# One PSUM accumulation and one quotient per attention head, in a fused attention and channel-mix kernel

## The chip, the cores and the metric

The kernel runs on one core of a Trainium2 chip. The metric is the device time of one execution in microseconds; lower is better. Engines are named as the profile names them: PE (TensorE matmuls) with PEld (its weight loads), DVE (VectorE), ACT (ScalarE), POOL (GpSimd) and SP (SyncE, which issues the DMAs).

## The reference

Attention for 8 batches of 8 heads, with 1152 keys of width 64. Neighbouring queries are averaged in twos, so each head has 576 queries. The heads of a batch, side by side, are the 576 x 512 input of a gated channel mix.

```python
def _attn_ref(q, k, v):                       # each 8 x 8 x 1152 x 64
    q_pool = q.reshape(B, H, S // 2, 2, D).mean(axis=3)
    scores = 1.0 / np.sqrt(D) * np.matmul(q_pool, k.transpose(0, 1, 3, 2))
    scores = scores - np.max(scores, axis=-1, keepdims=True)
    attn = np.exp(scores)
    attn = attn / (np.sum(attn, axis=-1, keepdims=True) + 1e-09)
    return np.matmul(attn, v)

def _moe_ref(x, mu_k, mu_r, w_k, w_v, w_r):   # x: 8 x 576 x 512
    x_prev = x shifted by one row of the sequence, zeros first
    xk = mu_k * x + (1.0 - mu_k) * x_prev
    xr = mu_r * x + (1.0 - mu_r) * x_prev
    k = np.maximum(xk @ w_k, 0.0)             # 512 x 1024
    v = k * k @ w_v                           # 1024 x 512
    return 1.0 / (1.0 + np.exp(-(xr @ w_r))) * v
```

## The kernel before

The 64 heads are worked off one after the other. `prep` loads k, q and v of a head and splits each into two float16 parts (tiles kn, qn, vt, vb). `block` handles 96 queries, six blocks to a head: scores of all 1152 keys into one of three PSUM tiles `s` (PE, L356), the maximum over keys (DVE `mx` L363, PE L366, DVE `mb` L369, PE L371, ACT L374), a second scores product that corrects the first and takes the maximum off (PE, L380), the exponential into `pf` (ACT, L386), and its low part into `pl` (POOL, L388).

`window` multiplies the exponentials with v. A group is 128 queries; the five groups of a head start at 0, 128, 256, 352 and 448 (the last ones overlap). Each group is 27 matmuls that accumulate in 65 columns of PSUM tile `a`, one bank: nine of L404, nine of L406 (high parts) and nine of L411 (low parts). Column 64 becomes the sum of the exponentials, the divisor. Before the change the five groups form three windows, `WIN`: groups 0 and 1 are issued after block 2, groups 2 and 3 after block 4, group 4 after block 5. Each window ends with a quotient of its own on DVE: `den` = divisor plus a guard (L427), its reciprocal (L429), and the product `xb` (L430). After the odd head of a pair each window is also turned: PE transposes one 128 x 128 block per group into bank `a` (L440), and ACT copies the result to `xt` (L444), the channel mix's input. Bank `a` is one buffer: the next group, quotient or transpose that uses it waits for the last.

`ff` is the channel mix for 256 rows at a time: `mix` makes xk and xr (ACT L510, DVE L513 and L518), then come its matmuls (PE, L538). A pair of heads is one of the four pieces of 128 channels over which its first products sum, so it starts as the pairs of a batch are turned, and runs interleaved with the heads of later batches. `weights` splits the three weight matrices, 20 pieces, by four DVE instructions each (L471 to L475); in the trace the last of them runs at 202 us.

Nothing is issued where it is written. `op` records each step with its engine, an assumed duration, the buffers it reads and writes, and a key; `Issue.run` then plays the whole list forwards and backwards with these durations and latencies and fixes one order per engine. So a change in a few steps changes the order everywhere.

Of the kernel before, what the change touches and what calls it, by code (L numbers as in the profile page):

```python
# [10 lines left out]
F32 = mybir.dt.float32  # L11
# [22 lines left out]
GUARD = 1e-9 * math.exp(SHIFT) * 2.0 ** -40  # L34
# [6 lines left out]
O_MAX, O_EXP, O_REST, O_AV, O_EVAC, O_TURN = -6.0, 0.0, 3.0, 14.0, 6.0, 4.0  # L41
# [134 lines left out]
def kernel(  # L176
# [65 lines left out]
    vb = bufs("vb", NV, [P, NC, D + 2], F16)  # L242
    pf = const.tile([P, NC, TQ], I32, name="pf")
    pl = const.tile([P, NC, TQ], F16, name="pl")
    mx, mb = bufs("mx", 3, [P, QN], F16), bufs("mb", 3, [P, 1], F16)
    den, xb = bufs("den", 2, [P, 2], F32), bufs("xb", NW, [P, 2, 2, D], F32)
    xt = bufs("xt", 3, [P, NG, TQ + 1], F32)
    xm = {n: const.tile([P, NG, T], F32, name=f"x{n}") for n in "kr"}
    xl = {n: const.tile([P, NG, T], F16, name=f"xl{n}") for n in "kr"}
# [10 lines left out]
    a_b = psum.tile([P, 512], F32, name="a")  # L260
# [130 lines left out]

    def window(n, w, t):

        b, h = divmod(n, H)
        g, hh = divmod(h, 2)
        starts, r1, _ = WIN[w]
        m = len(starts)
        jv = n % NV
        VN = D + 1
        vk = [(x, jv, c0) for x in ("vt", "vtl") for c0 in (0, 5)]  # L400

        def hi(a0, rows, c0, c1, first):
            for c in range(c0, c1):
                nc.tensor.matmul(a_b[:, a0:a0 + VN], half(pf, F16, 1)[:, c, rows], vt[jv][:, c, D:D + VN],  # L404
                                 start=(first and c == 0), stop=False, skip_group_check=True)
                nc.tensor.matmul(a_b[:, a0:a0 + D], half(pf, F16, 1)[:, c, rows], vt[jv][:, c, 0:D],  # L406
                                 start=False, stop=False, skip_group_check=True)

        def lo(a0, rows, c0, c1):
            for c in range(c0, c1):  # L410
                nc.tensor.matmul(a_b[:, a0:a0 + VN], pl[:, c, rows], vb[jv][:, c, 0:VN],  # L411
                                 start=False, stop=(c == NC - 1), skip_group_check=True)

        for k_, r0 in enumerate(starts):
            js = range(r0 // QN, (r0 + P - 1) // QN + 1)
            a0, rows = k_ * VN, slice(r0, r0 + P)
            for c0 in (0, 3, 6):
                op("PE", 3 * 0.0595, lambda a0=a0, rows=rows, c0=c0, first=(k_ == 0): hi(a0, rows, c0, c0 + 3, first),
                   r=vk + [("pf", j) for j in js] + ([("a",)] if c0 or k_ else []), w=[("a",)], key=t)
            for c0, c1 in ((0, 5), (5, NC)):  # L420
                op("PE", (c1 - c0) * 0.030, lambda a0=a0, rows=rows, c0=c0, c1=c1: lo(a0, rows, c0, c1),
                   r=[("vb", jv)] + [("pl", j) for j in js] + [("a",)], w=[("a",)], key=t)

        u = a_b[:, 0:m * VN].rearrange("p (k x) -> p k x", k=m)
        z = iss.nx = 1 - getattr(iss, "nx", 0)
        dz, xz = den[z][:, 0:m], xb[w][:, 0:m]
        op("DVE", 0.13, lambda: nc.vector.tensor_scalar(dz, u[:, :, D], GUARD, None, op0=ALU.add),  # L427
           r=[("a",)], w=[("den", z)], key=t + O_EVAC)
        op("DVE", 0.1, lambda: nc.vector.reciprocal(dz, dz), r=[("den", z)], w=[("den", z)], key=t + O_EVAC)  # L429
        op("DVE", 0.13 + m * D / 960, lambda: nc.vector.tensor_tensor(  # L430
            xz[:, :, hh], u[:, :, 0:D], dz.unsqueeze(2).broadcast_to([P, m, D]), op=ALU.mult),
           r=[("den", z), ("a",)], w=[("xb", w, hh)], key=t + O_EVAC)
        if hh == 0:
            return
        q0 = r1 - starts[0]
        qe = starts[-1] + P - starts[0]

        def turned():
            for k_, r0 in enumerate(starts):
                nc.tensor.transpose(a_b[:, r0 - starts[0]:r0 - starts[0] + P],  # L440
                                    xz[:, k_].rearrange("p h d -> p (h d)"), ident)

        op("PE", 0.11 * m, turned, r=[("xb", w, 0), ("xb", w, 1)], w=[("a",)], key=t + O_TURN)
        op("ACT", 0.051 + (qe - q0) / 1200, lambda: nc.scalar.copy(  # L444
            xt[b % 3][:, g, 1 + r1:1 + r1 + qe - q0], a_b[:, q0:qe]),
           r=[("a",)], w=[("xt", b % 3, g, w)], key=t + O_TURN)
# [49 lines left out]
    def mix(w, t0, t1, key, dk):  # L496

        m, o = mu[w]
        n = t1 - t0
        hi = top(xm[w])  # L500
        for c in range(NG):
            t = t0
            while t < t1:
                b = t // TQ
                e = min(t1, (b + 1) * TQ)
                x, s0, ln, o0 = xt[b % 3], t - b * TQ, e - t, t - t0
                z = turn("tmp")
# [5 lines left out]
                op("DVE", ln / 960 + 0.069, lambda x=x, s0=s0, ln=ln, o0=o0, z=z, c=c: nc.vector.scalar_tensor_tensor(  # L513
                    xm[w][:, c, o0:o0 + ln], x[:, c, s0 + 1:s0 + 1 + ln], m[:, c:c + 1], tmp[z][:, 0:ln],
                    op0=ALU.mult, op1=ALU.add),
                   r=xk + [("tmp", z)], w=[("x", w, c, t > t0)], key=key + c * dk)
# [152 lines left out]
```

## Time and profile before

| | before |
|---|---|
| median of three runs | 1249.62 us (1249.33 to 1250.01) |
| the profiled execution's own time | 1250.17 us |
| span of the profile | 1248.4 us, so 1.8 us lie around it |
| busy PE, DVE | 1160.0 us (93%), 1027.8 us (82%) |
| busy ACT, POOL | 855.7 us (69%), 537.6 us (43%) |
| DVE instructions L427, L429, L430 | 192 each |
| ACT copies L444, PE transposes L440 | 96, 160 |

A row of a group names line, engine, operation, output and inputs, shapes and count; behind the bar stand busy us and mean ns of one, then the engine's idle time just before and what ended it. A row of waits names who waited for whom, the total in us, how many times, and the longest. A row of the timeline has start, duration, and what ran. A busy time includes the end of an instruction while the next is already running, so what an instruction takes from its queue is read from the starts of two rows that follow each other without idle time between.

### The profile page before, as it was taken

Reading aid. Unit: us, or ns where it says so; the run is one execution under the profiler, and the core shown is the slowest. Engines: PE = TensorE matmul, PEld = TensorE weight load, DVE = VectorE, ACT = ScalarE, POOL = GpSimd, SP = SyncE. Lnnn points to the kernel's source line nnn. Section 1 sums busy time; section 2 is a strip of 40 time slices with the busy share of each in tenths; the row PEclk is TensorE's granted clock in tenths of the full one; section 3 lists DMA queues with packets and bytes.
Section 4 is the critical chain, followed back from the end, with each engine's and each line's share of the span. In section 5 each row is a group of like instructions: output and inputs, shape, how many; then the busy total and the mean of one; then the engine's idle time right before and its main releaser. Section 6 shows DMA issues by size and latency. Waiting matters only on the chain.

```text
span 1248.4 us, 46035 instructions
## 1 busy us (share of the span) xinstructions
PE 1160.0 (93%) x19504; PEld 933.6 (75%) x19504; DVE 1027.8 (82%) x2297; ACT 855.7 (69%) x1769; POOL 537.6 (43%) x548
## 2 busy tenths in 40 slices
PE   4687779999999999999999999999999999999998
PEld 3576666878778787878787787878787877878655
DVE  8999999989888988889888888788889788876441
ACT  5666677777767777677767677776777777756442
POOL 3556555444434444444544454544344443533111
PEclk9899999999999999999999999999999999999999
DMA  9566446645444454345454555345545443230000
GB/s 231 156 147 157 105 123 145 158 96 121 90 100 98 114 115 96 91 98 127 85 121 83 114 97 115 84 103 107 104 105 101 106 97 72 58 67 3 19 24 26
DMA packets 222319, 126.71 MB, mean 102 GB/s; under 512 B 157600, under 2 KB 194464, under 8 KB 222112
## 3 DMA queue, kind: packets, MB, share of 16 engines
q1 hardware_dynamic: 222112, 123.77, 44.4%
q8 instruction: 152, 2.49, 0.8%
q14 instruction: 55, 0.45, 0.1%
HBM read 67.11 MB, written 9.44 MB: 61 GB/s over the span
## 4 chain that ended last, share of the span: by engine, by line
PE 54%; DVE 28%; ACT 9%; issue 6%; DMA 2%; POOL 0%; SPq 0%; ACTq 0%; DVEq 0%
PE f L538 19%; DVE mx L363 9%; PE s L380 7%; PE s L356 6%; PE a L411 4%; PE a L404 4%; PE a L406 4%; PE s L538 4%; ACT pf L386 3%; DVE mb L369 2%; DVE vt L331 2%; DVE qn L318 2%; DVE xk L513 2%; DVE xr L513 2%; PE s L366 2%
## 5 line engine op out<-in xcount | busy, mean ns | idle before, releaser
L388 POOL TENSOR_SCALAR pl<-pf 128x864 f16<-128x864 uint16 x384 | 380.5, 991 | 489.1 <-ACT pf L386 441.4
L363 DVE TENSOR_REDUCE mx<-s 128x96 f16<-128x864 f32 x384 | 397.6, 1048 | 51.1 <-PE s L356 46.5
L386 ACT ACTIVATE pf<-s 128x864 int32<-128x864 f32 x384 | 338.1, 890 | 110.7 <-PE s L380 74.2
L356 PE MATMUL s<-qT,ks 128*128 128x96 f16 x3456 | 218.7, 207 | 23.6 <-DMA qT<-qn 14.6
L404 PE MATMUL a<-vt,pf 128*128 128x65 f16 x2880 | 234.4, 194 | 3.4 <-DVE xb L430 2.4
L406 PE MATMUL a<-vt,pf 128*128 128x64 f16 x2880 | 234.7, 194 | 0.0
L380 PE MATMUL s<-qT,ks 128*128 128x96 f16 x3456 | 219.8, 208 | 8.8 <-ACT qT L374 6.3
L356 PEld LDWEIGHTS <-ks 128*128 128x128 f16 x3456 | 187.7, 99 | 49.8 <-issue 14.8
L380 PEld LDWEIGHTS <-ks 128*128 128x128 f16 x3456 | 185.5, 99 | 38.1 <-issue 15.2
L404 PEld LDWEIGHTS <-pf 128*128 128x128 f16 x2880 | 203.5, 99 | 4.7
L406 PEld LDWEIGHTS <-pf 128*128 128x128 f16 x2880 | 193.9, 98 | 13.4 <-issue 5.3
L374 ACT ACTIVATE qT<-s 1x96 f16<-1x96 f32 x384 | 92.0, 243 | 127.7 <-PE s L371 117.0
L411 PE MATMUL a<-vb,pl 128*128 128x65 f16 x2880 | 152.9, 194 | 0.0
L538 PE MATMUL f<-xk,wk_hi 128*128 128x256 bf16 x496 | 136.4, 275 | 2.3 <-ACT r L565 2.1
L538 PE MATMUL f<-xk,wk_lo 128*128 128x256 bf16 x496 | 136.7, 276 | 0.0
L538 PE MATMUL f<-xlk,wk_hi 128*128 128x256 f16 x496 | 134.2, 271 | 0.0
L569 POOL TENSOR_TENSOR gl<-g 128x512 f16<-128x512 f32 x72 | 79.0, 1098 | 127.0 <-ACT g L567 125.6
L369 DVE TENSOR_REDUCE mb<-s 96x1 f16<-96x128 f32 x384 | 108.3, 282 | 23.5 <-PE s L366 20.5
L411 PEld LDWEIGHTS <-pl 128*128 128x128 f16 x2880 | 122.2, 99 | 1.9
L538 PEld LDWEIGHTS <-wk_hi 128*128 128x128 f16 x1152 | 105.6, 97 | 15.7 <-issue 2.9
L366 PE MATMUL s<-identb,mx 128*96 128x128 f16 x384 | 90.4, 235 | 22.4 <-DVE mx L363 21.0
L371 PE MATMUL s<-negi,mb 96*128 96x96 f16 x384 | 80.8, 211 | 19.5 <-DVE mb L369 12.1
(90 smaller groups left out, 2075.7 us busy)
## 6 DMA issues: line engine op xcount, KB each, us to landing
kr<-in_k_dram SPq DMA_DIRECT2D x64, 288.0 KB, 3.3
qr<-in_q_dram SPq DMA_DIRECT2D x64, 288.0 KB, 3.2
vr<-in_v_dram SPq DMA_DIRECT2D x64, 288.0 KB, 3.0
ks<-ks SPq DMA_DIRECT2D x64, 144.0 KB, 3.1
out_dram<-em SPq DMA_DIRECT2D x36, 256.0 KB, 2.3
st<-in_moe_w_k_dram SPq DMA_DIRECT2D x8, 512.0 KB, 4.5
st<-in_moe_w_v_dram SPq DMA_DIRECT2D x8, 512.0 KB, 3.6
st<-in_moe_w_r_dram SPq DMA_DIRECT2D x4, 512.0 KB, 3.8
```

Source lines behind the costliest of these rows:

```text
L356: nc.tensor.matmul(cols(c, c + 1), ks1[hp][:, c, :], qT[hp][:, j, 0, :], start=(c == c0), stop=False, skip_group_check=True)
L363: op("DVE", 0.967, lambda: nc.vector.tensor_reduce(mxz, grid(0, NC).rearrange("p c q -> p q c"), axis=AX.X, op=ALU.max), r=[("s", z)], w=[ ...
L366: op("PE", 0.054, lambda: nc.tensor.matmul(s[0:QN, 0:P], mxz, identb, start=False, stop=False, skip_group_check=True), r=[("mx", z)], w=[( ...
L369: op("DVE", 0.199, lambda: nc.vector.tensor_reduce(mbz[0:QN], s[0:QN, 0:P], axis=AX.X, op=ALU.max), r=[("s", z)], w=[("mb", z)], key=t + O ...
L374: op("ACT", 0.133, lambda: nc.scalar.activation(qT[hp][QN:QN + 1, j, 1, :], s[QN:QN + 1, 0:QN], AF.Prelu, scale=1.0 - EPS, alpha=(1.0 + EP ...
L380: nc.tensor.matmul(cols(c, c + 1), ks2[hp][:, c, :], qT[hp][:, j, 1, :], start=False, stop=True, skip_group_check=True)
L386: op("ACT", NC * QN / 1200 + 0.051, lambda: nc.scalar.activation(pf[:, :, rows], grid(0, NC), AF.Exp, bias=SHIFT, scale=0.125 / (2.0 * SQ) ...
L388: op("POOL", NC * QN / 1000 + 0.066, lambda: nc.gpsimd.tensor_scalar(pl[:, :, rows], half(pf, U16, 0)[:, :, rows], LO, 1.0, op0=ALU.mult, ...
L404: nc.tensor.matmul(a_b[:, a0:a0 + VN], half(pf, F16, 1)[:, c, rows], vt[jv][:, c, D:D + VN], start=(first and c == 0), stop=False, skip_gr ...
L406: nc.tensor.matmul(a_b[:, a0:a0 + D], half(pf, F16, 1)[:, c, rows], vt[jv][:, c, 0:D], start=False, stop=False, skip_group_check=True)
L411: nc.tensor.matmul(a_b[:, a0:a0 + VN], pl[:, c, rows], vb[jv][:, c, 0:VN], start=False, stop=(c == NC - 1), skip_group_check=True)
L538: nc.tensor.matmul(ps, terms[i][0], terms[i][1], start=(first and i == 0), stop=(i == last), skip_group_check=True)
```

## The change

All five groups of a head accumulate side by side in bank `a` (5 x 65 = 325 of 512 columns); group k is issued after block k + 1. One quotient per head follows the fifth group, over five divisors and 320 columns. After the odd head the transposes come in two pieces, `TURN`: groups 0 to 2 with a copy of 384 columns, then groups 3 and 4 with a copy of 192 columns, through the same bank. Tile `xb` is one buffer in place of three. The recorded durations of the DVE steps change too: 0.075, 0.08 and 0.403 us for a head, against 0.13, 0.1 and 0.13 + 0.067 per group for a window.

```diff
-    WIN = [((0, 128), 0, 2), ((256, 352), 256, 4), ((448,), 480, 5)]
+    WIN = [(0, 1), (128, 2), (256, 3), (352, 4), (448, 5)]
...
+    TURN = [(0, 3, 0), (3, 5, 384)]
...
-    den, xb = bufs("den", 2, [P, 2], F32), bufs("xb", NW, [P, 2, 2, D], F32)
+    den, xb = bufs("den", 2, [P, NW], F32), bufs("xb", 1, [P, NW, 2, D], F32)
...
+        a0, rows = w * VN, slice(r0, r0 + P)
...
-                                 start=(first and c == 0), stop=False, skip_group_check=True)
+                                 start=(w == 0 and c == 0), stop=False, skip_group_check=True)
...
+        if w < NW - 1:
+            return
+
+        u = a_b[:, 0:NW * VN].rearrange("p (k x) -> p k x", k=NW)
+        z = n % 2
+        dz, xz = den[z], xb[0]
+        op("DVE", 0.075, lambda: nc.vector.tensor_scalar(dz, u[:, :, D], GUARD, None, op0=ALU.add),
            r=[("a",)], w=[("den", z)], key=t + O_EVAC)
-        op("DVE", 0.1, lambda: nc.vector.reciprocal(dz, dz), r=[("den", z)], w=[("den", z)], key=t + O_EVAC)
-        op("DVE", 0.13 + m * D / 960, lambda: nc.vector.tensor_tensor(
-            xz[:, :, hh], u[:, :, 0:D], dz.unsqueeze(2).broadcast_to([P, m, D]), op=ALU.mult),
-           r=[("den", z), ("a",)], w=[("xb", w, hh)], key=t + O_EVAC)
+        op("DVE", 0.08, lambda: nc.vector.reciprocal(dz, dz), r=[("den", z)], w=[("den", z)], key=t + O_EVAC)
+        op("DVE", 0.07 + NW * D / 960, lambda: nc.vector.tensor_tensor(
+            xz[:, :, hh], u[:, :, 0:D], dz.unsqueeze(2).broadcast_to([P, NW, D]), op=ALU.mult),
+           r=[("den", z), ("a",)], w=[("xb", hh)], key=t + O_EVAC)
         if hh == 0:
             return
...
+        for k0, k1, q0 in TURN:
+            base = WIN[k0][0]
+            qe = WIN[k1 - 1][0] + P
+
+            def turned(k0=k0, k1=k1, base=base):
+                for k_ in range(k0, k1):
+                    r_ = WIN[k_][0] - base
+                    nc.tensor.transpose(a_b[:, r_:r_ + P], xz[:, k_].rearrange("p h d -> p (h d)"), ident)
+
+            op("PE", 0.11 * (k1 - k0), turned, r=[("xb", 0), ("xb", 1)], w=[("a",)], key=t + O_TURN)
+            op("ACT", 0.051 + (qe - q0) / 1200, lambda q0=q0, qe=qe, base=base: nc.scalar.copy(
+                xt[b % 3][:, g, 1 + q0:1 + qe], a_b[:, q0 - base:qe - base]),
+               r=[("a",)], w=[("xt", b % 3, g, k0)], key=t + O_TURN)
```

In the changed kernel the lines of these steps are: `mx` L364, `mb` L370, `den` L429, reciprocal L431, `xb` L432, the group's matmuls L407, L409 and L414, the transposes L444, their copies L447, the scores L357 and L381, and the mix's matmuls L541.

The first place is DVE in the ninth head (the trace of before has these rows from 184.19 us on). Beside the quotient's tiles there are `kn` and `qn` of a later head's preparation and the maxima `mx` and `mb` of blocks. Before, its first window's quotient and the start of the second's:

```order
L427 TENSOR_SCALAR den_103<-a 128x2
L301 TENSOR_TENSOR kn_78<-kr_70,kn_78 128x5x64
L429 RECIPROCAL den_103<-den_103 128x2
L363 TENSOR_REDUCE mx_98<-s_134 128x96
L430 TENSOR_TENSOR xb_104<-a,den_103 128x2x64
L301 TENSOR_TENSOR kn_78<-kr_70,kn_78 128x4x64
L369 TENSOR_REDUCE mb_101<-s_134 96x1
L363 TENSOR_REDUCE mx_96<-s_132 128x96
L318 SCALAR_TENSOR_TENSOR qn_80<-qs_76,qn_80 96x3x64 x2
L427 TENSOR_SCALAR den_102<-a 128x2
L369 TENSOR_REDUCE mb_99<-s_132 96x1
L429 RECIPROCAL den_102<-den_102 128x2
```

After, the only quotient of the same head, with steps of the weights (`ex`), of v (`vt`) and of q (`qs`) beside it:

```order
L370 TENSOR_REDUCE mb_100<-s_131 96x1
L429 TENSOR_SCALAR den_102<-a 128x5
L332 SCALAR_TENSOR_TENSOR vt_88<-vr_73,vt_88 128x4x64
L431 RECIPROCAL den_102<-den_102 128x5
L310 TENSOR_TENSOR qs_77<-qr_75 96x384
L432 TENSOR_TENSOR xb_104<-a,den_102 128x5x64
L364 TENSOR_REDUCE mx_98<-s_132 128x96
L302 TENSOR_TENSOR kn_79<-kr_71,kn_79 128x5x64
```

Three quotients in a head (the third, of one group, stands after the second) have become one at its end, and other work still stands between its three steps.

The second place is ACT in the fourth pair of heads, where the turned blocks are copied. Before, the last two of the pair's three copies, with exponentials (`pf`), rows for the second product (`qT`), the channel mix's steps (`tmp`, `ex`, `em`) and v (`vt`) between them:

```order
L444 COPY xt_108<-a 128x224
L510 ACTIVATE tmp_119<-xt_107,omu_r 128x64
L586 ACTIVATE ex_120<-f 128x512
L588 ACTIVATE em_122<-f 128x512
L590 ACTIVATE ex_120<-ex_120 128x512
L386 ACTIVATE pf<-s_133 128x9x96
L374 ACTIVATE qT_86<-s_134 1x96
L591 ACTIVATE em_122<-em_122 128x512
L328 ACTIVATE vt_89<-vr_72 128x5x64
L444 COPY xt_108<-a 128x96
```

After, both copies of such a pair:

```order
L447 COPY xt_106<-a 128x384
L375 ACTIVATE qT_86<-s_132 1x96
L513 ACTIVATE tmp_116<-xt_106,omu_k 128x192
L387 ACTIVATE pf<-s_131 128x9x96
L447 COPY xt_106<-a 128x192
```

Three copies spread over the odd head have become two close together behind its end, with one exponential between them.

The third place is PE at the same pair of the changed kernel, just before the second piece is transposed. `ks` and `qT` belong to the scores of block tile `s_131`, `xr` and `wr_hi` to the channel mix:

```order
L381 LDWEIGHTS ks_0_84
L381 MATMUL s_131<-qT_86,ks_0_84 128x96
L541 LDWEIGHTS xr
L541 MATMUL f<-wr_hi,xr 128x512
L367 LDWEIGHTS mx_96
L367 MATMUL s_130<-identb,mx_96 96x128
L444 MATMUL a<-ident,xb_104 128x128 x2
```

Between the two pieces (the first stands 26 rows up) PE has 13 matmuls to do: the one of `mb` (L372), two of the channel mix with 512 columns, nine of L381 and the one of `mx` shown. Before, three pieces of two, two and one transposes stood far apart, with groups of the next window between them.

More of the change, by code (lines that the diff above doesn't have):

```diff
@@ L199 @@
     T = 256
-    WIN = [((0, 128), 0, 2), ((256, 352), 256, 4), ((448,), 480, 5)]
+    WIN = [(0, 1), (128, 2), (256, 3), (352, 4), (448, 5)]
     NW = len(WIN)
-    assert D == 64 and DM == NG * P and TQ == NB * QN == WIN[-1][0][-1] + P
+    TURN = [(0, 3, 0), (3, 5, 384)]
+    assert D == 64 and DM == NG * P and TQ == NB * QN == WIN[-1][0] + P
     const = ctx.enter_context(tc.tile_pool(name="const", bufs=1))
@@ L395, in window @@
         g, hh = divmod(h, 2)
-        starts, r1, _ = WIN[w]
-        m = len(starts)
+        r0 = WIN[w][0]
         jv = n % NV
@@ L400, in window, with hi, lo @@
         vk = [(x, jv, c0) for x in ("vt", "vtl") for c0 in (0, 5)]
-        def hi(a0, rows, c0, c1, first):
+        js = range(r0 // QN, (r0 + P - 1) // QN + 1)
+        a0, rows = w * VN, slice(r0, r0 + P)
+        def hi(c0, c1):
             for c in range(c0, c1):
                 nc.tensor.matmul(a_b[:, a0:a0 + VN], half(pf, F16, 1)[:, c, rows], vt[jv][:, c, D:D + VN],
-                                 start=(first and c == 0), stop=False, skip_group_check=True)
+                                 start=(w == 0 and c == 0), stop=False, skip_group_check=True)
                 nc.tensor.matmul(a_b[:, a0:a0 + D], half(pf, F16, 1)[:, c, rows], vt[jv][:, c, 0:D],
                                  start=False, stop=False, skip_group_check=True)
-        def lo(a0, rows, c0, c1):
+        def lo(c0, c1):
             for c in range(c0, c1):
@@ L412, in lo @@
                                  start=False, stop=(c == NC - 1), skip_group_check=True)
[L414 to L427, printed above, removed]
+        for c0 in (0, 3, 6):
+            op("PE", 3 * 0.0595, lambda c0=c0: hi(c0, c0 + 3),
+               r=vk + [("pf", j) for j in js] + ([("a",)] if c0 or w else []), w=[("a",)], key=t)
+        for c0, c1 in ((0, 5), (5, NC)):
+            op("PE", (c1 - c0) * 0.030, lambda c0=c0, c1=c1: lo(c0, c1),
+               r=[("vb", jv)] + [("pl", j) for j in js] + [("a",)], w=[("a",)], key=t)
@@ L433, in window @@
+        op("DVE", 0.07 + NW * D / 960, lambda: nc.vector.tensor_tensor(
+            xz[:, :, hh], u[:, :, 0:D], dz.unsqueeze(2).broadcast_to([P, NW, D]), op=ALU.mult),
+           r=[("den", z), ("a",)], w=[("xb", hh)], key=t + O_EVAC)
         if hh == 0:
             return
[L435 to L446, printed above, removed]
+        for k0, k1, q0 in TURN:
[9 more added lines that the diff above has]
+               r=[("a",)], w=[("xt", b % 3, g, k0)], key=t + O_TURN)
@@ L507, in mix @@
                 z = turn("tmp")
-                xk = [("xt", b % 3, c, w_) for w_, (st_, r1, _) in enumerate(WIN)
-                      if r1 < s0 + ln and st_[-1] + P > s0 - 1]
+                xk = [("xt", b % 3, c, k0) for k0, k1, q0 in TURN
+                      if q0 < s0 + ln and WIN[k1 - 1][0] + P > s0 - 1]
                 op("ACT", ln / 1200 + 0.187, lambda x=x, s0=s0, ln=ln, z=z, c=c: nc.scalar.activation(
@@ L622 @@
             block(n, j, i, i * PER)
-            for w, (_, _, after) in enumerate(WIN):
+            for w, (_, after) in enumerate(WIN):
                 if after == j:
```

## The prediction

> **What bounds it now.** I read the page's busy times and slices first, then the stretches, the chain, the waits, and last single rows.
>
> ```profile
> PE 1160.0 (93%) x19504; PEld 933.6 (75%) x19504; DVE 1027.8 (82%) x2297; ACT 855.7 (69%) x1769; POOL 537.6 (43%) x548
> ...
> PE   4687779999999999999999999999999999999998
> ...
> DVE  8999999989888988889888888788889788876441
> ```
>
> PE is the busiest, but not from the start: over the first six slices (31 us each) PE has 4 to 8 tenths while DVE has 8 to 9. So I cut the span at 20, 240 and 1160 us. Columns: stretch, its length, then busy us of PE, PEld, DVE, ACT and POOL, clock, DMA.
>
> ```profile
> 20.00:240.00 220.00, 178.84 (x3228) 149.43 (x3225) 211.46 (x446) 155.70 (x313) 117.53 (x110) 0.95 0.60 146
> 240.00:1160.00 920.00, 892.69 (x15718) 730.36 (x15719) 769.96 (x1754) 654.24 (x1365) 400.68 (x416) 1.00 0.44 96
> 1160.00:1248.00 88.00, 84.60 (x524) 50.50 (x522) 29.79 (x58) 37.74 (x75) 12.70 (x12) 1.00 0.07 24
> ```
>
> From 20 to 240 us DVE is busy 211.46 of 220 us (96%) and PE idles 41.2. From 240 to 1160 us PE is busy 97% and idles 27.3, with DVE at 84%. In the last 88 us only the channel mix is left, on PE. The chain of each of the two long stretches says the same:
>
> ```profile
> by line: DVE mx L363 20.6%; issue 12.4%; DVE mb L369 4.6%; DVE ex L473 4.3%; DVE kn L301 4.2%; PE s L380 4.2%; ACT pf L386 4.0%; DVE qn L318 3.5%; DVE vt L331 3.5%; DVE ex L475 3.4%; PE a L404 2.7%; DVE ex L471 2.5%; PE a L406 2.5%; PE a L4
> ...
> by line: PE f L538 23.1%; PE s L380 8.9%; PE s L356 8.1%; DVE mx L363 7.3%; PE a L411 5.3%; PE a L404 5.1%; PE a L406 5.0%; issue 5.0%; ACT pf L386 3.8%; DVE xk L513 2.3%; DVE mb L369 2.0%; PE s L366 1.9%; DVE xr L513 1.8%; DVE vt L331 1.7%
> ```
>
> DVE leads the first, PE the second. How PE stands behind DVE and ACT in the first stretch, and then in the second:
>
> ```profile
> PE s L366 <- DVE mx L363: 13.5, 21, 1.8
> ...
> PE s L371 <- DVE mb L369: 5.3, 14, 0.7
> ...
> PE s L371 <- DVE den L427: 3.0, 4, 1.0
> ...
> PE a L404 <- DVE xb L430: 2.4, 4, 0.9
> ...
> PE a L404 <- ACT xt L444: 0.8, 3, 0.4
> ```
>
> ```profile
> DVE den L427 <- PE a L411: 38.5, 44, 2.6
> ...
> PE s L371 <- DVE mb L369: 6.8, 19, 0.7
> PE s L366 <- DVE mx L363: 6.5, 18, 0.7
> ...
> PE s L371 <- DVE den L427: 3.5, 6, 1.1
> ```
>
> PE waits on DVE 24.2 us of the first 220 (11.0%) and 16.8 of the 920 (1.8%). The first row of the second fence is the opposite case: DVE stands 44 times at a quotient whose group PE has not finished, with the maxima of later blocks queued behind.
>
> **Step 1, fewer DVE instructions.** The ninth head's first quotient, and the one-group quotient of its last window:
>
> ```profile
> 184.19 0.14 DVE L427 TENSOR_SCALAR den<-a 128x2 f32<-128x2 f32 x1
> 184.26 0.47 DVE L301 TENSOR_TENSOR kn<-kr,kn 128x320 f16<-128x320 f32 x1
> 184.66 0.15 DVE L429 RECIPROCAL den<-den 128x2 f32<-128x2 f32 x1
> 184.74 1.03 DVE L363 TENSOR_REDUCE mx<-s 128x96 f16<-128x864 f32 x1
> 185.69 0.27 DVE L430 TENSOR_TENSOR xb<-a,den 128x128 f32<-128x128 f32 x1
> 185.89 0.40 DVE L301 TENSOR_TENSOR kn<-kr,kn 128x256 f16<-128x256 f32 x1
> ...
> 195.39 0.21 DVE L430 TENSOR_TENSOR xb<-a,den 128x64 f32<-128x64 f32 x1
> 195.52 1.04 DVE L363 TENSOR_REDUCE mx<-s 128x96 f16<-128x864 f32 x1
> ```
>
> By starts, a quotient takes 0.07 (den) + 0.08 (reciprocal) from the queue, and xb 0.20 for 128 columns or 0.13 for 64, so 0.07 per 64 columns; 320 columns make 0.20 + 3 x 0.07 = 0.41. A head took 2 x 0.35 + 0.28 = 0.98 and will take 0.56: 0.42 less. The five-element den and reciprocal I price as the two-element ones. By durations the same steps cost, in the two stretches (all rows that touch den, three to a quotient):
>
> ```profile
> 20.00:240.00 220.00, 18.82 (x102) 0.95 0.60 146
> 240.00:1160.00 920.00, 90.64 (x474) 1.00 0.44 96
> ```
>
> That is 34 and 158 quotients, or 11.3 and 52.7 heads. A head after is 0.14 + 0.15 + 0.27 + 3 x 0.07 = 0.77 to 0.80 by durations, so the second figures are 18.8 - 9.0 = 9.8 us and 90.6 - 42.1 = 48.5 us less busy.
>
> First stretch: DVE is the bound, so what its queue saves comes off: 11.3 x 0.42 = **4.7 us**. The bounds are 0 (PE's idle goes to something else) and 9.8 (durations). I take the starts, since nearly every step there has its successor running in its end.
>
> The Trainium skill, Perfetto Trace Analysis, section Optimizing Scalar/DVE Operations, gives each DVE instruction a fixed cost of about 60 ns on SBUF and 125 ns on PSUM. By that, a head loses two den, two reciprocals and two xb, an estimate of 0.62 us, and this term would be 7.0. The trace disagrees for PSUM: den reads bank `a` and gives up its slot after 70 ns.
>
> Second stretch: PE is the bound and only its waits can go. DVE loses 52.7 x 0.42 = 22 us of slots, 2.4 points of 920. Between the two stretches PE's waits on DVE rise sixfold (1.8% to 11.0%) over 12.4 points of DVE load; on that slope (a logarithm, my choice) 2.4 points take away 30% of 16.8: **5.0 us**. By durations it is 5.3 points and 9 us. The ends are 0 and all 16.8. Fewer quotients also mean fewer places where DVE stands for PE: at the old rate of 44 in 158, 53 quotients stand 15 times, 13 us in place of 38.5. I give that no term of its own; it supports the 5.0.
>
> **Step 2, bank `a` changes hands differently.** A quotient before held the bank three times a head, now once but longer: xb's slot grows by 0.21. From the order I sum PE's work between a quotient's last L411 (now L414) and the next user of the bank, with PE's paces as rows show them (the first row: nine scores matmuls in 0.54, the last 0.2 of it drain, so 0.042 each; the next two: 0.22 for 512 columns).
>
> ```profile
> 249.57 0.54 PE L356 MATMUL s<-qT,ks 128*128 128x96 f16 x9
> ...
> 1190.56 0.38 PE L538 MATMUL s<-wv_hi,g 128*128 128x512 f16 x1
> 1190.78 0.38 PE L538 MATMUL s<-wv_lo,g 128*128 128x512 f16 x1
> ```
>
> The least is 1.3 us and the median 2.6 (before: 0.5 and 2.3), against a drain of 0.2, the quotient's 0.56, about 0.1 of handovers (an estimate from the copy's below) and what stands between the three DVE steps. Cost 0: the cover grew. Were it gone, each of 64 quotients would cost up to 0.9.
>
> The transposes are new in that two pieces follow closely. One handover from 246.54 us on, and ACT's copies by width, with the exponential that may stand ahead of one:
>
> ```profile
> 246.54 0.38 PE L440 MATMUL a<-ident,xb 128*128 128x128 f32 x2
> ...
> 246.95 0.35 ACT L444 COPY xt<-a 128x224 f32<-128x224 f32 x1 [0.22 <-PE a L440]
> ...
> 247.43 0.19 PE L404 MATMUL a<-vt,pf 128*128 128x65 f16 x1
> ```
>
> ```profile
> L386 ACT ACTIVATE pf<-s 128x864 int32<-128x864 f32 x384 | 338.1, 890 | 110.7 <-PE s L380 74.2
> ...
> L444 ACT COPY xt<-a 128x256 f32<-128x256 f32 x32 | 11.7, 367 | 4.0 <-PE a L440 3.4 <-DVE kn L301 0.4
> ...
> L444 ACT COPY xt<-a 128x96 f32<-128x96 f32 x32 | 7.6, 237 | 5.3 <-PE a L440 5.1
> ```
>
> Copies cost 0.81 ns a column beyond 0.16 us: 0.47 for 384 columns, 0.32 for 192. Two transposes take 0.11 each to issue (0.38 less the 0.27 of a single one's drain), so from 246.76 to the copy's end at 247.30 pass 0.54 us; with 0.05 for the release (an estimate, between 0 and the 0.13 to the L404 row) 0.59 for 224 columns, so 0.72 before the second piece and 0.56 before the next head's group. The work between, in the order's piece shown above, is 0.05 + 2 x 0.22 + 9 x 0.042 + 0.06 = 0.91. Over all 32 pairs four fall short before the second piece and four before the next head, 2.1 us together; by the same count the old order was short 1.6. Cost **0.5 us**; the ends are -1.6 and the slower rival's price below. ACT's total falls from 0.95 to 0.79 a pair; it is not the bound (71% at most): 0.
>
> **Step 3, groups issued earlier.** Matmuls, exponentials and transposes (160) stay as many: 0 on PE. What changes is when `pf` and `pl` are read out; the mix's matmuls (23% of the chain) fill PE meanwhile. One `xb` buffer in place of three: the next pair's first quotient comes after a whole head of groups in the same bank, so it waits for nothing new. The last head: the order has eight mix matmuls ahead of the first of its two pieces and seven between them; 0.
>
> **Sum.** 1250.17 - 4.7 - 5.0 + 0.5 = 1241.0 in the profiled execution, which stands 0.55 above the median of the runs: 1240.5.
>
> **Rivals.**
> *More.* Both stretches follow durations: -9.8 - 9 + 0.5 gives 1231; with every wait of the second gone (-16.8), 1223. For it: PE's idle beyond the named waits (41.2 against 24.2) may shrink with them. Against it: DVE steps overlap at their ends.
> *Nothing.* The whole order is made anew, and DVE's slots are saved where PE is not behind DVE: 17 of its 41 idle us in the first stretch have other names. Then 1249.6. Against it: DVE's 96%.
> *Slower.* ACT lets one exponential (0.89) pass ahead of the 384-column copy, and PE, which works in order, stands at the second piece. Cover 0.91 less need 0.72 leaves 0.70 us a pair, 22 us, and 1263. It eats the gain from 0.29 us a pair on, and is slower by over 0.2% from 0.37. For it: the copies now are close together at the busiest place, where the old ones were spread. Against it: PE waited only 0.8 us for ACT's copies in the first stretch, and copies mostly waited for PE (3.4 and 5.1 in the two rows).
> Beside that rival stands the Trainium skill, Perfetto Trace Analysis, section Optimizing Tensor Performance (Matmuls): independent groups should rotate through PSUM banks, so that the evacuation of one overlaps the next one's matmuls. By that rule, gathering five groups in one bank speaks against the change; the trace so far bears out little of it, since L404 waited 2.4 us for xb.
>
> **Chances.** My forecast (1235 to 1246) 0.50, more 0.20, nothing 0.18, slower 0.12. A measurement here can tell 0.2%, 2.5 us, from no change; so faster 0.70, same 0.18, slower 0.12. The range 1227 to 1252 holds the forecast, most of "more", and "nothing".
>
> **What would show it.** Right: 64 rows each of den, reciprocal and xb, xb near 0.5; PE's idle in the first 240 us down by about 5; the eighth head's end earlier by some 3 us; waits of den for PE near a third of 38.5; almost none of L444 for `xt`. Wrong: PE's waits for ACT `xt` above 10 us, or DVE's busy share in the first stretch unchanged with the same heads done.

## The result: slower by 1%, and the profile after

The changed kernel takes 1259.70 us (median of four runs, 1258.52 to 1262.88), the kernel before 1249.47 beside it. The ratio is 1.0096 (95% interval 1.0077 to 1.0115; the quotient of the two medians is 1.0082). By the medians it is slower by 10.2 us, where 1240.5 was forecast and 1252 was the range's upper end. The profiled execution took 1258.52 us with a span of 1256.4, 8.0 us more than the span before.

The page's busy times and slices:

```profile
PE 1161.8 (92%) x19504; PEld 933.9 (74%) x19504; DVE 998.8 (79%) x1913; ACT 856.8 (68%) x1737; POOL 540.5 (43%) x548
...
PE   4787888999999999999999999999999999999998
...
DVE  8999999889688878789688878787888788775441
```

DVE has 384 instructions and 29.0 busy us less, as the change says (the forecast's 0.42 of queue time a head makes 26.9), and PE the same matmuls and 1.8 us more. The kernel is slower though no engine has 3 us more to do. The stretches, cut as before (length, busy us of PE, PEld, DVE, ACT and POOL, clock, DMA):

```profile
20.00:240.00 220.00, 183.37 (x3374) 157.34 (x3375) 212.27 (x392) 158.64 (x316) 130.97 (x113) 0.92 0.63 151
240.00:1160.00 920.00, 881.62 (x15480) 717.04 (x15478) 738.75 (x1417) 649.65 (x1325) 390.57 (x412) 1.00 0.43 94
1160.00:1256.00 96.00, 92.64 (x620) 55.95 (x616) 31.23 (x65) 39.26 (x78) 12.70 (x12) 1.00 0.06 23
```

In the first stretch PE idles 36.6 us in place of 41.2 and runs 146 more matmuls, even at a clock of 0.92 where it was 0.95. In the second PE idles 38.4 us in place of 27.3 and runs 238 matmuls fewer, which are left for the end. To put both on one scale I give each matmul its own pace (0.216 us for 512 columns, 0.042 for 96, and so on, from starts of rows that follow each other without idle time; 1074.9 us in all) and add up what is done. By 240 us the changed kernel has done 150.2 us of PE work, before 143.2: 7.0 ahead. From 240 to 1100 us it does 776.6 against 791.0: 14.4 lost. The difference, 7.4, is nearly the 8.0 of the spans. So in this pair the first stretch went as forecast, and the loss is all in the second, where the granted clock is 1.00 in both kernels.

Whom PE waits for in the second stretch:

```profile
PE s L372 <- DVE mb L370: 17.4, 41, 1.1
PE s L367 <- DVE mx L364: 12.1, 36, 1.1
...
PE a L407 <- ACT xt L447: 0.3, 1, 0.3
PE a L444 <- DVE xb L432: 0.2, 1, 0.2
```

The waits for `mb` and `mx`, 6.8 and 6.5 us before, are 17.4 and 12.1. Bank `a` and the copies, on which the forecast's slower rival rested, cost 0.5 us. And for whom DVE waits there:

```profile
DVE mx L364 <- PE s L357: 65.6, 58, 4.5
DVE mb L370 <- PE s L367: 37.0, 85, 0.8
```

DVE has more time to spare than before and is late for PE more often. Both engines wait for each other at the same chain: block's maximum `mx` (DVE), its transpose (PE, L367), `mb` (DVE), the matmul that spreads it (PE, L372), `qT` (ACT), the second scores (PE, L381), the exponential (ACT). One such wait, of PE (start, duration, what ran, and in brackets idle before it):

```profile
811.55 0.26 PE L367 MATMUL s<-identb,mx 128*96 128x128 f16 x1 [0.38 <-DVE mx L364]
811.64 0.38 PE L541 MATMUL f<-wr_hi,xlr 128*128 128x512 f16 x1
811.86 0.38 PE L541 MATMUL f<-wr_hi,xr 128*128 128x512 f16 x1
812.08 0.38 PE L357 MATMUL s<-qT,ks 128*128 128x96 f16 x5
812.29 0.38 PE L541 MATMUL f<-wr_lo,xr 128*128 128x512 f16 x1
813.72 0.22 PE L372 MATMUL s<-negi,mb 96*128 96x96 f16 x1 [1.05 <-DVE mb L370]
```

with DVE at the same time:

```profile
811.42 0.86 DVE L332 SCALAR_TENSOR_TENSOR vt<-vr,vt 128x256 f16<-128x256 f32 x1
812.21 1.25 DVE L516 SCALAR_TENSOR_TENSOR xk<-xt,mu_k,tmp 128x256 f32<-128x256 f32 x1
813.39 0.28 DVE L370 TENSOR_REDUCE mb<-s 96x1 f16<-96x128 f32 x1
```

and POOL:

```profile
811.10 0.91 POOL L389 TENSOR_SCALAR pl<-pf 128x864 f16<-128x864 uint16 x1 [1.70 <-ACT pf L387]
812.09 1.09 POOL L572 TENSOR_TENSOR gl<-g 128x512 f16<-128x512 f32 x1
```

The written order gives DVE two 256-column steps between a block's `mx` and its `mb`. In the planner's durations each is 256/960 + 0.069 = 0.34 us; here they hold the queue for 0.79 and 1.18, so `mb` starts 1.3 us later than planned. PE had four short pieces of other work listed ahead of L372, then stood for 1.05 us.

### The profile page after: what moved, and what is told of

Same layout as the page of the kernel before. It is cut to its first block, busy times and chain, and to the rows that moved or that the text cites. A ratio compares the mean times of both kernels' runs of the same rounds, so it can differ in the third digit from the quotient of the medians.

```text
span 1256.4 us, 45576 instructions
## 1 busy us (share of the span) xinstructions
PE 1161.8 (92%) x19504; PEld 933.9 (74%) x19504; DVE 998.8 (79%) x1913; ACT 856.8 (68%) x1737; POOL 540.5 (43%) x548
## 4 chain that ended last, share of the span: by engine, by line
PE 48%; DVE 31%; ACT 10%; issue 7%; DMA 3%; SPq 0%; DVEq 0%; ACTq 0%
PE f L541 17%; DVE mx L364 10%; PE s L381 6%; PE s L357 5%; PE s L541 4%; ACT pf L387 4%; PE a L414 3%; PE a L407 3%; PE a L409 3%; DVE vt L332 3%; DVE mb L370 2%; DVE xk L516 2%; DVE xr L516 2%; DVE kn L302 2%; DMA qT<-qn 2%
## 5 line engine op out<-in xcount | busy, mean ns | idle before, releaser
L389 POOL TENSOR_SCALAR pl<-pf 128x864 f16<-128x864 uint16 x384 | 385.0, 1003 | 500.9 <-ACT pf L387 481.8
L364 DVE TENSOR_REDUCE mx<-s 128x96 f16<-128x864 f32 x384 | 399.9, 1048 | 82.5 <-PE s L357 65.8
L357 PE MATMUL s<-qT,ks 128*128 128x96 f16 x3456 | 225.4, 209 | 21.9 <-DMA qT<-qn 14.0
L407 PE MATMUL a<-vt,pf 128*128 128x65 f16 x2880 | 237.2, 194 | 1.6 <-ACT xt L447 1.4
L409 PE MATMUL a<-vt,pf 128*128 128x64 f16 x2880 | 237.4, 194 | 0.0
L357 PEld LDWEIGHTS <-ks 128*128 128x128 f16 x3456 | 189.0, 99 | 49.1 <-DMA ks<-kn 13.0
L381 PE MATMUL s<-qT,ks 128*128 128x96 f16 x3456 | 217.0, 209 | 8.4 <-ACT qT L375 6.8
L381 PEld LDWEIGHTS <-ks 128*128 128x128 f16 x3456 | 184.2, 99 | 34.8 <-issue 17.6
L407 PEld LDWEIGHTS <-pf 128*128 128x128 f16 x2880 | 204.0, 99 | 5.4
L409 PEld LDWEIGHTS <-pf 128*128 128x128 f16 x2880 | 193.8, 98 | 12.1 <-issue 2.4
L414 PE MATMUL a<-vb,pl 128*128 128x65 f16 x2880 | 155.0, 194 | 0.3 <-POOL pl L389 0.3
L370 DVE TENSOR_REDUCE mb<-s 96x1 f16<-96x128 f32 x384 | 108.2, 282 | 45.1 <-PE s L367 42.2
L541 PE MATMUL f<-xk,wk_hi 128*128 128x256 bf16 x496 | 136.9, 276 | 3.9 <-ACT r L568 3.9
L541 PE MATMUL f<-xk,wk_lo 128*128 128x256 bf16 x496 | 137.0, 276 | 0.0
L541 PE MATMUL f<-xlk,wk_hi 128*128 128x256 f16 x496 | 134.5, 271 | 0.7 <-DVE xlk L521 0.7
L414 PEld LDWEIGHTS <-pl 128*128 128x128 f16 x2880 | 123.0, 99 | 4.9 <-POOL pl L389 0.4
L541 PEld LDWEIGHTS <-wk_hi 128*128 128x128 f16 x1152 | 105.4, 97 | 16.8 <-issue 4.4
L367 PE MATMUL s<-identb,mx 128*96 128x128 f16 x384 | 91.0, 237 | 22.9 <-DVE mx L364 21.2
L372 PE MATMUL s<-negi,mb 96*128 96x96 f16 x384 | 81.5, 212 | 29.1 <-DVE mb L370 28.2
```

Of the source, the lines that this page charges most:

```text
L357: nc.tensor.matmul(cols(c, c + 1), ks1[hp][:, c, :], qT[hp][:, j, 0, :], start=(c == c0), stop=False, skip_group_check=True)
L364: op("DVE", 0.967, lambda: nc.vector.tensor_reduce(mxz, grid(0, NC).rearrange("p c q -> p q c"), axis=AX.X, op=ALU.max), r=[("s", z)], w=[ ...
L367: op("PE", 0.054, lambda: nc.tensor.matmul(s[0:QN, 0:P], mxz, identb, start=False, stop=False, skip_group_check=True), r=[("mx", z)], w=[( ...
L370: op("DVE", 0.199, lambda: nc.vector.tensor_reduce(mbz[0:QN], s[0:QN, 0:P], axis=AX.X, op=ALU.max), r=[("s", z)], w=[("mb", z)], key=t + O ...
L381: nc.tensor.matmul(cols(c, c + 1), ks2[hp][:, c, :], qT[hp][:, j, 1, :], start=False, stop=True, skip_group_check=True)
L389: op("POOL", NC * QN / 1000 + 0.066, lambda: nc.gpsimd.tensor_scalar(pl[:, :, rows], half(pf, U16, 0)[:, :, rows], LO, 1.0, op0=ALU.mult, ...
```

## The experiments

What the runs had to tell apart were five explanations. *Slack*: the planner fills the time that DVE saved so tightly that a late step has nothing to absorb it. *Lottery*: any two lists of this planner differ by some microseconds. *Issue*: groups issued one per block (k + 1) space the blocks differently. *Bank*: the one quotient and its bank. *Margin*, which took over from slack: the planner counts with handovers between engines that the chip has only at best, and the changed kernel's list leaves less room on the chain of a block.

The table has all runs. "Room" is the mean time, from 240 to 1160 us, from the start of a block's `mx` to the start of its exponential, worked out from the trace's records, so that it holds both what the list planned and how late the steps were; the waits are PE's of that stretch, and the last column is PE work done from 240 to 1100 us. Each ratio is to the kernel before on the same chip.

| kernel | us | ratio (95%) | room | waits for mb, mx | PE work |
|---|---|---|---|---|---|
| before | 1249.5 | | 4.55 | 6.8, 6.5 | 791.0 |
| changed | 1259.7 | 1.0096 (1.0077 to 1.0115) | 4.18 | 17.4, 12.1 | 776.6 |
| before, shaken (b_jit1) | 1254.6 | 1.0053 (1.0034 to 1.0073) | 4.59 | 9.2, 7.1 | 790.1 |
| changed, shaken (a_jit1) | 1264.2 | 1.0123 (1.0103 to 1.0143) | 4.17 | 12.9, 13.6 | 777.5 |
| changed, quotient padded (a_pad) | 1255.1 | 1.0049 (1.0030 to 1.0068) | 4.22 | 12.3, 11.2 | 785.3 |
| before, quotients trimmed (b_tight) | 1255.1 | 1.0049 (1.0031 to 1.0066) | 4.53 | 6.2, 11.9 | 787.1 |
| changed, groups as before (a_win) | 1252.3 | 1.0028 (1.0015 to 1.0041) | 4.39 | 12.0, 10.6 | 786.0 |
| before, groups one per block (b_fine) | 1255.8 | 1.0059 (1.0039 to 1.0079) | 4.45 | 7.1, 9.9 | 786.8 |
| before, 0.3 (b_lat) | 1240.5 | 0.9932 (0.9909 to 0.9955) | 4.98 | 5.5, 7.3 | 795.9 |
| changed, 0.3 (a_lat) | 1243.9 | 0.9958 (0.9943 to 0.9974) | 4.74 | 11.7, 5.1 | 793.7 |
| before, 0.3 shaken (b_latj) | 1240.8 | 0.9942 (0.9919 to 0.9965) | 5.05 | 6.6, 6.9 | 797.0 |
| changed, 0.3 shaken (a_latj) | 1244.3 | 0.9968 (0.9949 to 0.9988) | 4.71 | 11.0, 7.4 | 797.3 |
| before, 0.4 (b_lat2) | 1243.7 | 0.9957 (0.9941 to 0.9973) | 5.43 | 6.5, 2.4 | 794.5 |
| changed, 0.4 (a_lat2) | 1234.7 | 0.9892 (0.9875 to 0.9910) | 5.15 | 6.8, 2.6 | 804.4 |
| before, 0.4 shaken (b_lat2j) | 1240.8 | 0.9946 (0.9931 to 0.9961) | 5.41 | 5.9, 4.3 | 795.2 |
| changed, 0.4 shaken (a_lat2j) | 1234.6 | 0.9896 (0.9880 to 0.9913) | 5.08 | 3.9, 1.7 | 803.2 |
| changed, 0.5 (a_lat3) | 1238.5 | 0.9925 (0.9911 to 0.9940) | 5.68 | 4.8, 1.1 | 803.9 |

**Durations of the quotient, and the shaken lists.** First the quotient's recorded durations alone, which change the written order and no instruction: longer in the changed kernel (a_pad), and the changed kernel's short ones in the kernel before (b_tight).

```diff
# a_pad, the changed kernel
-        op("DVE", 0.075, ... tensor_scalar(dz, ...
+        op("DVE", 0.2, ...
-        op("DVE", 0.08, ... reciprocal ...
+        op("DVE", 0.2, ...
-        op("DVE", 0.07 + NW * D / 960, ...
+        op("DVE", 0.27 + NW * D / 960, ...
# b_tight, the kernel before: 0.13 -> 0.075, 0.1 -> 0.08, 0.13 + m * D / 960 -> 0.07 + m * D / 960
```

> The changed kernel, with the durations that the planner is told for the three DVE steps of a quotient raised from 0.075, 0.08 and 0.403 to 0.2, 0.2 and 0.603 us (1.00 in place of 0.56 a head). The instructions are the same, only their order is listed anew. Theory 'slack': the old list counted 1.41 us a head for quotients whose slots take 0.98, so it carried 0.43 us a head of spare DVE time, and the new list carries none; then this run gives the spare time back and lands at 1238 to 1249. Theory 'bank': five groups in one bank with one quotient hold the bank too long, whatever the list; then 1256 to 1262. Theory 'lottery': any new list of 10,000 steps lands some 8 us to either side; then it tells nothing by itself.

> The kernel before, with the recorded durations of its quotient steps cut from 0.13, 0.1 and 0.13 + columns to the change's 0.075, 0.08 and 0.07 + columns. Nothing else. Slack: it loses the spare 0.43 us a head and becomes slower, 1254 to 1262. Bank: 1247 to 1252, since its windows and quotients are the old ones. Lottery: anywhere from 1241 to 1258.

And both kernels with every recorded duration changed by up to 2% either way, the same pattern in both: another list, in which nothing else is different.

```diff
+        dur *= 1.0 + 0.02 * (((n * 7919 + 1) * 104729 % 1009) / 504.0 - 1.0)
         self.ops.append((eng, dur, fn, key, deps))
```

> The changed kernel with every recorded duration of the planner shaken by up to 2% either way, mean zero: a new list with the same spare time. Slack and bank: 1256 to 1263, as unshaken. Lottery: off by 4 us or more.

> The kernel before with every recorded duration shaken by up to 2% either way, mean zero. Slack and bank: 1246 to 1253, as unshaken. Lottery: off by 4 us or more, then most likely slower, since the unshaken list was the one kept.

A shaken list costs the kernel before 6.7 us (1254.6 against 1247.9 on that chip): the lottery is real, and before's own list is a good draw. The changed kernel's ratio goes from 1.0096 to 1.0123, with intervals that overlap. But shaken against shaken, on one chip, the changed kernel is still 9.6 us slower (1264.2 - 1254.6), so the lottery, as far as two lists of each kernel can tell, does not explain the 10.2.

For slack the two runs disagree. The trimmed quotients landed in its 1254 to 1262 (1255.1), but shaking alone costs as much, so that run does not tell the two apart. The padded ones missed its 1238 to 1249: 1255.1, just below the 1256 to 1262 of bank. Padding took the changed kernel's ratio from 1.0096 to 1.0049, an amount that the shaking could also give.

The waits of the two shaken lists in the second stretch; first before's, then the changed kernel's (one line was added ahead of these, so its lines count one higher):

```profile
PE s L372 <- DVE mb L370: 9.2, 23, 1.0
PE s L367 <- DVE mx L364: 7.1, 19, 0.8
```

```profile
PE s L368 <- DVE mx L365: 13.6, 33, 1.3
PE s L373 <- DVE mb L371: 12.9, 31, 1.0
```

The difference of the originals, 13.3 against 29.5 us, stands again as 16.3 against 26.5.

**Where the groups are issued.** The changed kernel with its groups issued as before (0 and 1 after block 2, and so on), the one quotient kept:

```diff
# a_win, the changed kernel
-    WIN = [(0, 1), (128, 2), (256, 3), (352, 4), (448, 5)]
+    WIN = [(0, 2), (128, 2), (256, 4), (352, 4), (448, 5)]
```

> The changed kernel with its one quotient per head and its two-piece transposes, but the groups issued as before: 0 and 1 after block 2, 2 and 3 after block 4, 4 after block 5. Theory 'issue': one group per block spaces the blocks evenly and takes away the pairs of blocks that ran side by side, so that PE comes to each block's maxima too early; then this run is back at 1244 to 1252, with PE's waits for mb and mx from 240 to 1160 us near 17 in place of 29.5. Theory 'quotient' (one long hold of the bank): 1256 to 1263, waits near 30. Theory 'margin' (the list runs each block's chain of maxima closer, because DVE is less loaded): 1252 to 1260.

And the kernel before with one group per block, its three quotients kept:

```diff
# b_fine, the kernel before; window() handles group ks and returns ahead of the quotient unless last
-            for w, (_, _, after) in enumerate(WIN):
+            for w, ks, after, last in ((0, (0,), 1, False), (0, (1,), 2, True), (1, (0,), 3, False),
+                                       (1, (1,), 4, True), (2, (0,), 5, True)):
```

> The kernel before with its three windows and three quotients, but its groups issued one per block, after blocks 1, 2, 3, 4 and 5, as in the change. Issue: slower, 1255 to 1264, with PE's waits for mb and mx near 30 in the second stretch. Quotient and margin: 1247 to 1255, as a shaken list of the kernel before.

The old places took the changed kernel's ratio from 1.0096 to 1.0028 (7.4 us between the medians, which are of two chips), and room went from 4.18 to 4.39. The new places cost the kernel before 7.5 us, about as much as a shaken list. The waits of a_win, and then of b_fine:

```profile
PE s L372 <- DVE mb L370: 12.0, 29, 1.5
PE s L367 <- DVE mx L364: 10.6, 27, 1.3
```

```profile
PE s L366 <- DVE mx L363: 9.9, 29, 0.9
PE s L371 <- DVE mb L369: 7.1, 13, 0.7
```

With one quotient and the old places PE still waits 22.6 us, with three quotients and the new places 17.0. Issue had said near 17 for the first and near 30 for the second, so the waits deny it, though b_fine's time lies in its 1255 to 1264 and just above margin's 1255. The places seem to share in the loss but are not shown to be the cause by themselves. By the ratios the two halves of the change nearly add up: 0.0059 for the places (b_fine) and 0.0028 for the quotient, its bank and its two pieces (a_win) make 0.0087, against 0.0096 for both. Neither half is much larger than what a shaken list can cost.

**Room on the chain.** The last idea is that it matters what the planner believes of a handover. From its tables, and from the records of the second stretch (start to start; the lines are the changed kernel's):

| step | planner, at least | shortest, changed | mean, changed | mean, before |
|---|---|---|---|---|
| mx to PE L367 | 1.14 | 1.07 | 1.27 | 1.32 |
| PE L367 to mb | 0.25 | 0.25 | 0.53 | 0.51 |
| mb to PE L372 | 0.37 | 0.30 | 0.54 | 0.55 |
| PE L372 to qT | 0.25 | 0.24 | 0.42 | 0.42 |
| qT to the exponential | 0.89 | 0.93 | 1.41 | 1.75 |

What the planner counts for a handover is about the shortest that the chip does, in both kernels alike. The last two columns do not bear margin out as the difference between the kernels: from `mx` to `qT`, where the waits for `mx` and `mb` lie, a block takes 2.80 us before and 2.77 after. Nearly all of the room that was lost, 0.34 of 0.37 us, lies behind `qT`, where the exponential follows sooner. The start times that the planner itself gives the two lists, worked out from the two kernel files (blocks from 220 to 1060 us of its own time), say the same: 2.64 and 2.61 us from `mx` to `qT`, then 2.60 and 2.28 to the exponential. What runs can still test is whether more room takes the waits away.

Three latencies were raised, in the planner alone; no instruction differs. They count for every handover between these engines, not only for those of a block's chain.

```diff
-           ("PE", "ACT"): 0.2, ("PE", "DVE"): 0.2, ("DVE", "PE"): 0.17, ...
+           ("PE", "ACT"): 0.3, ("PE", "DVE"): 0.3, ("DVE", "PE"): 0.3, ...     # a_lat, b_lat
```

> The changed kernel with the planner's assumed latencies between PE and DVE, DVE and PE, and PE and ACT raised from 0.2, 0.17 and 0.2 to 0.3 us: the same instructions, with more room left in the list behind each step of a block's chain of maxima. Margin: the waits for mb and mx fall to 20 or less in the second stretch and the time to 1240 to 1252. Issue and quotient: waits stay near 30 and the time at 1255 to 1264.

> The same longer latencies in the kernel before, as control. Margin: its waits are already at 17, so a smaller gain or none, 1243 to 1253; the distance between the two kernels with longer latencies is then under 4 us. Issue and quotient: 1247 to 1255, with the changed one still 6 us or more behind.

Both kernels became faster than the kernel before, by 4 and 8 us on that chip, and the difference between them shrank from 10.2 to 3.4. The changed kernel's waits for `mb` and `mx` fell from 29.5 to 16.8 us. The waits of b_lat did not fall, 12.8 us against 13.3:

```profile
PE s L366 <- DVE mx L363: 7.3, 15, 1.3
PE s L371 <- DVE mb L369: 5.5, 12, 1.2
```

Yet it gained 7.7 us and landed below the 1243 to 1253 expected of it. So these waits are not the only way in which longer latencies pay, and the runs do not show the other. I went on to 0.4, and to 0.3 with shaken durations (another pattern than in a_jit1 and b_jit1):

```diff
+           ("PE", "ACT"): 0.35, ("PE", "DVE"): 0.4, ("DVE", "PE"): 0.4, ...    # a_lat2, b_lat2
```

> The changed kernel with still longer assumed latencies: PE to DVE and DVE to PE 0.4, PE to ACT 0.35 us. If margin is the cause, more of it takes away more of the waits for mb and mx (16.8 us with 0.3), until the list gets longer by its own account: 1238 to 1246. If the 0.3 list was a lucky one: 1250 or more.

> The kernel before with the same still longer latencies. Margin: 1238 to 1248, less to gain than the changed kernel, since DVE is fuller and the early stretch is bound by it. Luck: 1250 or more.

> The changed kernel with latencies of 0.3 us and every recorded duration shaken by up to 2%, mean zero. Margin: within 5 us of the unshaken one (1239 to 1249) and far below the changed kernel's own 1259.7. Luck: back to 1252 or more.

> The kernel before with latencies of 0.3 us and the same shaking. Margin: 1237 to 1249. Over three lists each with longer latencies the changed kernel and the one before then stand within 4 us of each other; if the change itself (bank, quotient, groups) costs time beyond its list, the changed one stays 5 us or more behind in all three.

At 0.4 the changed kernel takes 1234.7 us, faster than the 1238 to 1246 expected, 9.0 less than the kernel before with the same latencies, and 13.5 less than the kernel before as it was on that chip. Its second stretch:

```profile
240.00:1160.00 920.00, 896.19 (x15820) 738.99 (x15818) 742.71 (x1448) 663.70 (x1357) 401.35 (x418) 1.00 0.44 96
```

```profile
PE s L372 <- DVE mb L370: 6.8, 10, 1.2
PE s L381 <- ACT qT L375: 6.7, 14, 0.9
PE s L367 <- DVE mx L364: 2.6, 7, 0.6
```

PE idles 23.8 us in place of 38.4, with the same DVE instructions. The waits for `mb` and `mx` fell from 29.5 to 9.4; what is late next is `qT` on ACT, at 6.7. At 0.3 shaken the difference between the kernels is 3.5 us, where it was 3.4 unshaken.

Still open was whether the changed kernel's lead at 0.4 is its list's luck, and whether more room goes on paying:

```diff
+           ("PE", "ACT"): 0.45, ("PE", "DVE"): 0.5, ("DVE", "PE"): 0.5, ...    # a_lat3
# a_lat2j, b_lat2j: as a_lat2 and b_lat2, with every duration shaken by up to 2%
```

> The changed kernel with latencies of 0.4, 0.4 and 0.35 us, and every recorded duration shaken by up to 2%. Waits for mb and mx near the unshaken list's 9.4 us. If the change itself is worth time once the list has room: 1231 to 1240. If 1234.7 was a lucky list: 1241 to 1247, level with the kernel before at the same latencies (1243.7).

> The kernel before with the same latencies and the same shaking. If the change is worth time once the list has room: 1240 to 1247, 4 us or more behind the changed one. If 1243.7 was an unlucky list: 1234 to 1240.

> The changed kernel with latencies of 0.5, 0.5 and 0.45 us. Room beyond what the delays need is paid for in the list: the waits for mb and mx fall below 9 us but the time no longer: 1233 to 1243. If more room still pays: under 1232.

Shaken, the lead at 0.4 is 6.2 us (1234.65 against 1240.82), and the changed kernel is at 1234.65 again. At 0.5 it loses 3.8 of the gain. The waits of a_lat2j, and then of a_lat3:

```profile
PE s L382 <- ACT qT L376: 9.6, 16, 1.4
PE s L373 <- DVE mb L371: 3.9, 9, 0.8
...
PE s L368 <- DVE mx L365: 1.7, 5, 0.5
```

```profile
PE s L381 <- ACT qT L375: 11.1, 21, 1.7
PE s L372 <- DVE mb L370: 4.8, 7, 1.7
```

With enough room DVE's steps are late less often, and ACT's `qT` (the one handover of the three that I raised less) takes their place. By the profiles, what a_lat3 loses lies in the first stretch: 140.0 us of PE work done at 240 us, where a_lat2j has 147.2.

So the change, each time on lists made alike, costs 10.2 and 9.6 us with the old latencies, 3.4 and 3.5 with 0.3, and gains 9.0 and 6.2 with 0.4. That order holds in both draws at each setting. Two draws are few, but with raised latencies the two lists of one kernel lie within 2.9 us of each other (on different chips), which is less than the lead at 0.4.

## Why the prediction was wrong

**Step 1, first stretch (4.7 us off): held in this pair of lists.** The groups of the quotient, 64 instructions each:

```profile
L432 DVE TENSOR_TENSOR xb<-a,den 128x320 f32<-128x320 f32 x64 | 30.8, 481 | 0.7
...
L431 DVE RECIPROCAL den<-den 128x5 f32<-128x5 f32 x64 | 11.6, 181 | 0.8
L429 DVE TENSOR_SCALAR den<-a 128x5 f32<-128x5 f32 x64 | 10.0, 156 | 11.9 <-PE a L414 11.4
```

xb lasts 0.48, as forecast ("near 0.5"), and from start to start a quotient takes 0.56 to 0.59 (the 21 heads in which each of its three steps is followed without idle time), the forecast's 0.56 being the lower end. PE's idle fell by 4.6 (forecast: about 5), and PE work at 240 us is 7.0 ahead. Over the six pairs of lists made alike it is 7.0, 4.8, 4.6, -0.6, -1.7 and 2.0, a mean of 2.7, so the 4.7 lies inside what lists differ by and is not proven beyond this pair. One sign named for "wrong" half came true: DVE is as busy in this stretch as before (212.27 us, 211.46 before), but with more done, 12 heads' quotients in place of 11.3 and the weights finished at 192.6 us in place of 202.1. The eighth head's quotient ends 22.7 us earlier, not 3, since the new list has 6 matmuls of the channel mix ahead of it where there were 70; that sign was badly chosen.

**Step 1, second stretch (5.0 us off): this is the step that failed.** It read PE's waits for DVE as a function of how busy DVE is ("on that slope (a logarithm, my choice)"). DVE's busy share fell from 84% to 80%, as the step had it, and PE's waits for `mb` and `mx` rose from 13.3 to 29.5 us, PE's idle by 11. At unchanged DVE work the same waits fell from 29.5 to 9.4 us when nothing but the planner's latencies was raised (a_lat2 against the changed kernel): they follow from how the list is made, and not from the load alone. The term should have been about +14, the PE work lost between 240 and 1100 us. With 0.4 the term comes out with its forecast sign and more: 804.4 against 794.5, and 803.2 against 795.2 us of PE work, 9.9 and 8.0 us gained there. So the saved time is real, and at the old latencies the new list lost more than it. Why the changed kernel's list waits more than the old one at those latencies stays open. Room does not answer it: what was lost of it lies behind `qT`, and across the kernels it does not order the waits (a_lat has 4.74 us and waits 16.8, the kernel before has 4.55 and waits 13.3). a_pad and a_win each give part of the loss back, and neither effect is well above what a shaken list can do, up to 6.7 us.

The second half of that step, fewer places where DVE stands for PE, came true in its letter and not in its meaning: DVE's waits for a group to end fell from 38.5 to 6.9 us, below the third that was forecast (13), but the waits of its own `mx` and `mb` for PE rose from 45.4 and 16.4 to 65.6 and 37.0. They moved to the chain on which PE depends.

**Step 2, the bank (0.5 us): held.** Over the whole span PE waited 1.8 us for `xt` (L407 1.4, L444 0.4). The slower rival's mechanism was there in part: in 15 of the 32 pairs an exponential ran into the time between the first piece's transposes and its 384-column copy, which then started 0.37 to 1.54 us after the last transpose where 0.31 is the shortest. But PE had other matmuls listed and hardly stood, so the time came out on that rival's side by another way. (The work that it counted as 0.91 adds up to 0.93, which changes nothing. And the second and third place shown of the change are, by the trace, of the seventh pair of heads, at 276 us, not of the fourth.) The Trainium skill's rule to rotate groups through PSUM banks (Perfetto Trace Analysis, section Optimizing Tensor Performance) does not show in these waits as a cost, since the order puts other matmuls between the users of the bank. What the one bank does to the rest of the list is not told apart from the quotient (a_win).

**Step 3, the groups issued earlier (0 us): too small a question.** No matmul was added, as it said. But the places of the groups are part of what the planner works with, and a_win, which only puts them back, is 7.4 us faster. The rival "Nothing" named what mattered, "the whole order is made anew", and drew the wrong end from it: it took a new order to be neutral, when shaking alone cost the kernel before 6.7 us.

## What to carry to other kernels

Where an order is fixed ahead by a planner, its assumed handovers are part of the kernel: here, with handovers at the shortest the chip did, an edit that freed an engine came back as waits, and with longer ones it paid. So try an edit with latencies nearer the mean before judging it. Measure first what a new list alone does to the time (here up to 6.7 us for 2% on the durations), and compare edits on lists made alike. The version to keep here is the changed kernel with the 0.4 latencies, 1234.7 us, ratio 0.9892 (0.9875 to 0.9910).

## What the hardware showed that I had not expected

DVE steps that read SBUF can last up to nearly three times as long while POOL runs. In the changed kernel, of the 128x256 steps that make xk and xr, the 54 with no POOL instruction beside them have a median of 473 ns, the 42 with one 815 (worst 1378). The 320-column step of v has 481 and 890. It is not so whenever POOL runs: in the kernel before, the xk and xr steps with POOL beside them have medians of 476 and 475 (worst 1173). Steps that read a large operand from PSUM do not change: `mx` 1045 and 1046, xb 476 and 480. The group's row before, and then after:

```profile
L331 DVE SCALAR_TENSOR_TENSOR vt<-vr,vt 128x320 f16<-128x320 f32 x64 | 38.8, 607 | 3.5 <-ACT vt L328 3.4
```

```profile
L332 DVE SCALAR_TENSOR_TENSOR vt<-vr,vt 128x320 f16<-128x320 f32 x64 | 47.6, 744 | 1.2 <-ACT vt L329 0.8
```

Its mean rose by 137 ns with the step unchanged. Beside POOL stood 48 of the 64 before and 52 after, but the median of these rose from 522 to 890 ns: in the new order the 64 lie beside POOL for 65% of their time, where it was 51%, in part because a longer step meets more of it. The Trainium skill (Perfetto Trace Analysis, section Optimizing Scalar/DVE Operations) says that GpSimd and DVE share a read port of SBUF; these rows agree, but no run took POOL's work away, so the port as the cause, and such steps as the usual trigger of a late `mb`, stay argued. They do not explain the loss by themselves: all steps of v, xk and xr together last 169.5 us before and 188.1 after, but 176.0 and 181.7 on the shaken lists, where the loss is as large, and 178.4 in a_lat2. The planner's durations have no such case, and the row at 812.21 us, 1.25 where 0.34 was planned, is what it looks like.
